# Attention and MLP in one kernel: the second half of each unit issues transposed score, score, score, transposed score

## The chip, the cores and the metric

The kernel runs on one core of a Trainium2 chip. The metric is the device time of one execution in microseconds (us). The median of three timed runs of the kernel before is 1475.2 us (1474.68 to 1475.99). All profile readings here are of one profiled execution; TensorE is called PE, VectorE DVE, ScalarE ACT, GpSimd POOL and SyncE SP, as the profile does.

## The reference

```
xn  = layernorm(x)                                   # x: 2048 x 512
q, k, v = split(xn @ wqkv)                           # 32 heads of 16
o   = softmax(q k^T / sqrt(16)) v                    # 2048 x 2048 per head
A   = o @ wo
B   = gelu(xn @ w1 + b1) @ w2 + b2                   # 1792 hidden
out = x + A + B
```

Attention needs each score tile twice, once for the row maximum and once transposed for the exponential. The projections, the MLP and the output projection are dense products that fill the gaps of attention.

## The kernel before

Attention is cut into 512 units: a group of four heads (8 groups), a block of 512 queries (4 blocks), and 16 steps in each. The function `unit` issues one step. The array of PE is used as eight tiles of 64 rows by 32 columns: each product of 512 columns is sent as four matmuls for the four column groups (`tiled`, L169), on the lower rows (0 to 63) or the upper rows (64 to 127). Head b of the four lies on the lower rows when b is even and on the upper rows when b is odd. So two streams run side by side in the array, and the order in which the program lists them decides what stands in front of what.

A unit has two halves, a = 0 and a = 1. Each half first issues a quartet, then one value product and some dense products. The names used from here on, with the tile name of the profile in brackets:

- Sb, score of head b (`s_half`, tile pS): four matmuls of 62 rows, whose result DVE reduces to row maxima (`s_max`, L363). It takes the next of three score banks of PSUM in turn.
- Tb, transposed score of head b (`e_half`, tile pT): four matmuls of 64 rows, whose result ACT turns into exponentials (L410, tile pe). It takes the next bank from the list T, which it shares with the dense groups: four banks in all, of which a dense group holds one (D). When one dense group ends and the next begins, both hold one for a while, and T has two left.
- V, the value product (`v_half`, tile pV): four fp32 matmuls, one per head, each shown as two passes in the trace. In the half a = 0 it uses the upper rows (and exponentials of two units before), in the half a = 1 the lower rows (of the unit before).
- D, the dense products (`dense`, tile pD): on the rows that V leaves free, three or four products in a half. The pair of numbers is a group's pace: FAST is (4, 4), SLOW is (3, 3), MEAN is (3, 4), by even and odd units. The 56 hidden groups of the MLP have 12 products each and alternate SLOW and FAST; the second matrix of the MLP has MEAN and then FAST; the projections are FAST.

The order of a quartet is a table of pairs (kind, b), kind 1 for T and 0 for S. Before, the first half issues T1 (upper), S0 (lower), S1 (upper), T0 (lower), and the second S2 (lower), T3 (upper), S3 (upper), T2 (lower). After the first quartet V goes to the upper rows and D to the lower; after the second V goes to the lower and D to the upper. PE's instructions stand in exactly this order; a semaphore wait stands on the first matmul of an S (for DVE to have emptied its bank) or of a T (for ACT). V's first product waits for the V and D of the half before (`turns`, set in `enter` and `leave`). A dense group ends after a half a = 1, so the instruction of ACT that empties its bank (hh at L1312 for the hidden layer, pf at L604 for the projections) is issued after the first quartet of the next unit and before the second (`one_more`). `s_end` and `stores` turn a block's maxima once in 16 units, through PE (L386) and a bank of T.

Of the kernel before, what the change touches and what calls it, by code (L numbers as in the profile page):

```python
# [54 lines left out]
def layer_kernel(ctx: ExitStack, tc: tile.TileContext, x, wqkv, wo, w1, b1, w2, b2, out):  # L55
# [122 lines left out]
    def leave(user, goes_on):  # L178

        p = newest.pop(user, None)  # L180
        if p is not None and goes_on:
            p.then_inc(turns, 1)
            tc.no_tile_sem_insts.add(p.ins.name)
            counted[0] += 1
            left.append(p)

    def enter():

        if left:
            goal[0] = f"turn{counted[0]}"  # L190
            for p in left:
                tc.add_to_no_dep_group(goal[0], p.ins)
            left.clear()
# [16 lines left out]
    def fetch_scale(m):  # L210

        scale_of[m] = nc.scalar.alloc_register(f"sexp{m}")
        nc.scalar.reg_load(scale_of[m], sexp[0:1, m:m + 1].bitcast(I32))

    class Plan:
# [7 lines left out]
        def add(self, engine, ns, fn, after=(), take=(), free=(), size=0, tail=0, gap=0):  # L223
            t = dict(gap=gap, e=engine, ns=ns, fn=fn, after=[a for a in after if a], take=take, free=free, size=size, tail=tail,
                     end=None, n=len(self.todo))
            for key in free:
                self.users.setdefault(key, []).append(t)
            self.todo.append(t)
            return t
# [89 lines left out]
    def tick():  # L319
        held[0] = pos[0] < NU and pos[0] % 16 == 0  # L320
        run_due()
        run_steps()
        slot[0] += 1
# [42 lines left out]
    def s_half(u, n):  # L366

        s = banks("S")
        s_mm(u, n, s)
        s_max(u, n, s)  # L370

    def s_end(u):

        t, i = divmod(u, 16)
        if i < 15:
            return
        g, qb = divmod(t, NQB)
        mneg = mnegs[t % 2]
        nc.vector.tensor_reduce(mneg[:, :16], mt_of[t].rearrange("p h t k -> p (h t) k"), axis=AX.X, op=ALU.max, negate=True)
        given("dve", 220)  # L380

        def store():

            pt = banks("T")
            for a in range(2):
                nc.tensor.matmul(pt[32 * a:32 * a + 32, :64], mneg[64 * a:64 * a + 64, :],  # L386
                                 ident[64 * a:64 * a + 64, 64 * a:64 * a + 64], start=True, stop=True)
            mhl = work.tile([64, 2, 64], F16, name="mhl", bufs=2)
            nc.vector.tensor_scalar_mul(mhl[:, 0], pt[:64, :64], 1.0 / MROW)
            nc.vector.scalar_tensor_tensor(mhl[:, 1], pt[:64, :64], 1.0 / MROW, mhl[:, 0], op0=ALU.mult, op1=ALU.subtract)  # L390
            given("dve", 300)
            for a in range(2):
                nc.sync.dma_start(m_d[t, :, :, 64 * a:64 * a + 64], mhl[32 * a:32 * a + 16])
            for h in range(4):
                m_rows(t, h)

        stores[t] = store

    def e_half(u, n):

        p, a = divmod(n, 2)
        t, kt = divmod(u, 16)
        g, qb = divmod(t, NQB)
        st = banks("T")
        r = slice(64 * a, 64 * a + 64)
        k0 = (kt % 4) * P
        tiled(None, st, kst[g % 2][kt // 4][r, p, k0:k0 + P], qst[g % 2][qb][r, p, :], True, True)
        pe = work.tile([P, QB], F32, name="pe", bufs=12)
        ptiles[u, n] = pe
        nc.scalar.activation(pe, st, AF.Exp, scale=scale_of[g // 2])  # L410
        given("act", 520)

    def v_half(u, a):

        t, kt = divmod(u, 16)
        g, qb = divmod(t, NQB)
        if kt == 0 and a == 0:
            pv_of[t] = hold("V", "S")
        pv = pv_of[t][0]
        r = slice(64 * a, 64 * a + 64)  # L420
        for h in (2, 3, 0, 1):
            c = (4 * g + h) * VW
            product("V", pv[32 * h:32 * h + 32, :], vv[r, kt, c:c + 32], ptiles[u, h][r],
                    start=(kt == 0 and a == 0), stop=(kt == 15 and a == 1))
# [233 lines left out]
    def ended(at_once=True):  # L658

        if cur[0] is not None and cur[0].over():  # L660
            done, cur[0] = cur[0], None
            ends.append(done.end)
            if at_once:
                settle()
# [5 lines left out]
    def one_more():  # L670

        if ends:
            ends.pop(0)()
        elif extras:
            extras.pop(0)()
# [10 lines left out]
    def dense(gen, side):  # L686

        f = group(gen)
        for _ in range(0 if f is None else f.pace[pos[0] % 2]):
            if not f.usable(side):  # L690
                return
            f.product(side)
# [25 lines left out]
    def spare(gen, side):  # L718

        if extra[0] is None and not spent[0]:  # L720
            f = next(gen, 0)
            spent[0] = f == 0
            extra[0] = Halves(f) if f else None
        if extra[0] is not None:
            extra[0].product(side)
            if extra[0].at == extra[0].n:
                extra[0] = None
# [17 lines left out]
    def unit(gen):  # L745


        u = pos[0]
        e = u - LEAD
        if e > 0 and e % (2 * NQB * 16) == 0 and e < NU:  # L750
            fetch_scale(e // (2 * NQB * 16))
        pos[0] += 1
        for a in range(2):
            for kind, b in ((1, 1), (0, 0), (0, 1), (1, 0)) if a == 0 else ((0, 2), (1, 3), (0, 3), (1, 2)):
                if kind and 0 <= e < NU:
                    e_half(e, b)
                elif not kind and u < NU:
                    s_half(u, b)
                elif not kind and u > NU:
                    spare(gen, b % 2)  # L760
            if e >= 0:
                one_more()
                enter()

                w, r = (e - 2, 1) if a == 0 else (e - 1, 0)
                live = 0 <= w < NU
                new = r == 0 and w % 16 == 0
                if live and not new:
                    v_half(w, r)
                dense(gen, 1 - r)  # L770
                if live and new:
                    v_half(w, r)

                for user, goes_on in (("V", live and not (r == 1 and w % 16 == 15)),
                                      ("D", cur[0] is not None and not cur[0].over())):
                    leave(user, goes_on)
                for k in backlog:
                    backlog[k] = max(0, backlog[k] - HALF)
                if live and r == 1:
                    v_end(w)  # L780
                ended(False)

            if a == 0 and u % 16 == 0 and u // 16 - 1 in stores:
                stores.pop(u // 16 - 1)()
        if u < NU:
            s_end(u)
        tick()
# [9 lines left out]
    with ExitStack() as st1:  # L797
# [252 lines left out]
        for w in (1, 0):  # L1050
# [5 lines left out]
            else:  # L1056
                a = add("POOL", 800, lambda wf=wf, i1=i1: nc.gpsimd.tensor_scalar(tl[wf], tl[wf], i1, 0.0, op0=ALU.mult, op1=ALU.add), [h])
                w_ready[w] = add("POOL", 1100, lambda wf=wf, hi=hi, lo=lo: nc.gpsimd.tensor_tensor(lo, tl[wf], hi, op=ALU.subtract), [a], free=[wf])
        a = add("DVE", 90, lambda: nc.vector.tensor_tensor(sexp[:, 0:1], fac0[:, 0:1], fac0[:, 1:2], op=ALU.mult), [chain])
        a = add("DVE", 90, lambda: nc.vector.tensor_scalar_mul(sexp[:, 0:1], sexp[:, 0:1], DH ** -0.5), [a])  # L1060
# [5 lines left out]
        a = add("DVE", 90, lambda: nc.vector.tensor_tensor(amv[:, 2:3], amv[:, 0:1], amv[:, 1:2], op=ALU.max), v_sum)  # L1066
# [3 lines left out]
        for i in range(2):  # L1070
# [6 lines left out]
            else:  # L1077
                b = add("POOL", 1240, lambda key=key: nc.gpsimd.tensor_scalar(
                    tl[key], tl[key], inv_v[:, 0:1], 0.0, op0=ALU.mult, op1=ALU.add), [h])
# [30 lines left out]
        a = add("DVE", 220, maxima, m_last)  # L1110
# [3 lines left out]
        def turn_m():  # L1114
            tl[mkey] = sb_tile(mkey)
            for k in range(2):
# [3 lines left out]
        a = add("PE", 300, turn_m, [a], take=[mkey])  # L1120
        a = add("DVE", 160, lambda: nc.vector.tensor_scalar_mul(mhl[:, 0], tl[mkey][:64, :64], 1.0 / MROW), [a])
        a = add("DVE", 160, lambda: nc.vector.scalar_tensor_tensor(mhl[:, 1], tl[mkey][:64, :64], 1.0 / MROW, mhl[:, 0],
                                                                   op0=ALU.mult, op1=ALU.subtract), [a], free=[mkey])
# [136 lines left out]
        while not spent[0] or more or cur[0] is not None:  # L1260
            unit(fil)
            if pos[0] > 16:
                more = next(pre, 0) != 0
# [150 lines left out]
    with ExitStack() as st3:  # L1414
# [45 lines left out]
        while pos[0] < NU + LEAD + 2:  # L1460
            more_stacks()
            unit(fil)
# [32 lines left out]
```

## Time and profile before

| | |
|---|---|
| median of three timed runs | 1475.2 us |
| the profiled execution, its own time | 1476.9 us |
| its span | 1475.1 us |
| granted clock | 0.997 |
| ACT busy | 1260.5 us (85%) |
| POOL busy | 662.4 us (45%) |

The span runs from the first to the last instruction, and 1.8 us of the execution's own time lie outside it. Units run from about 99 us to 1460 us. In a timeline each row has the start and the length of one or several instructions that follow each other ("x4"); for PE a row of four matmuls with tile pS is one score, with pT one transposed score, and x8 two of them that overlap. A PE row's length is longer than the time for which the array is taken, since matmuls are pipelined; the spacing of starts on the same rows tells that time.

### The profile page before, as it was taken

To read this page: it belongs to the slowest core of one execution; us is meant where nothing else is said; L and a number is where in the kernel's file an instruction comes from. 1 tells how busy PE (TensorE), PEld (TensorE's weight loads), DVE (VectorE), ACT (ScalarE), POOL (GpSimd) and SP (SyncE) were. 2 spreads that over 40 slices of the span, in tenths; PEclk is the share of its full clock that TensorE was granted. 3 is DMA by queue.
4 is the path that set the end of the run, shared out by engine and by line. 5 is a ranking of instruction groups with operands and counts; after the bars stand their busy time and mean duration, and the time that the engine had idled before them with its cause. 6 is when DMAs were issued, how large, how long until landed. Compare 5 with 4: busy or idle time off the path is not lost.

```text
span 1475.1 us, 88125 instructions
## 1 busy us (share of the span) xinstructions
PE 1458.9 (99%) x40158; PEld 817.6 (55%) x40158; DVE 1356.4 (92%) x2305; ACT 1260.5 (85%) x2366; POOL 662.4 (45%) x672
## 2 busy tenths in 40 slices
PE   8999999999999999999999999999999999999998
PEld 4445555565555555555555555555555555555554
DVE  7889999999999999999999999999999999999933
ACT  5868888888999888899988889998889999888884
POOL 3201847563778401287830138783115777121100
PEclk9999999999999999999999999999999999999999
DMA  7732455545224210221113111121112110221432
GB/s 214 225 117 69 151 186 172 169 159 159 78 59 128 66 34 25 70 61 41 45 43 87 30 37 44 51 76 44 44 37 76 55 37 21 57 55 31 142 94 96
DMA packets 112623, 124.83 MB, mean 85 GB/s; under 512 B 22908, under 2 KB 84220, under 8 KB 112248
## 3 DMA queue, kind: packets, MB, share of 16 engines
q1 hardware_dynamic: 112248, 119.18, 27.0%
q8 instruction: 314, 5.14, 1.4%
q14 instruction: 61, 0.50, 0.1%
HBM read 81.66 MB, written 37.34 MB: 81 GB/s over the span
## 4 chain that ended last, share of the span: by engine, by line
PE 95%; ACT 2%; DVE 1%; DMA 1%; issue 0%; SPq 0%; DVEq 0%; ACTq 0%
PE pV L169 29%; PE pD L169 25%; PE pT L169 19%; PE pS L169 19%; PE pT L992 2%; DMA wq<-in_A_wqkv_dram 1%; PE pD L992 1%; DVE mt L363 1%; ACT pe L410 0%; DVE ac L1370 0%; DMA m_d<-mhl 0%; PE pT L962 0%; ACT xs L945 0%; ACT hh L1312 0%; PE pS L1158 0%
## 5 line engine op out<-in xcount | busy, mean ns | idle before, releaser
L363 DVE TENSOR_REDUCE mt<-pS 128x1 f32<-128x512 f32 x2029 | 1278.9, 684 | 54.9 <-PE pS L169 27.0
L410 ACT ACTIVATE pe<-pT 128x512 f32<-128x512 f32 x2048 | 1111.4, 599 | 168.1 <-PE pS L169 79.8
L169 PE MATMUL pV<-pe,vv 64*32 64x512 f32 x8192 | 1074.3, 594 | 0.1
L169 PE MATMUL pT<-qst,kst 64*32 64x512 f16 x8192 | 707.4, 377 | 2.0 <-issue 1.3
L169 PE MATMUL pS<-kst,qst 62*32 62x512 f16 x8116 | 611.1, 378 | 1.2 <-DVE mt L363 1.2
L169 PEld LDWEIGHTS <-qst 62*32 62x32 f16 x8192 | 286.0, 92 | 228.9 <-issue 55.3
L169 PE MATMUL pD<-xb,wc 64*32 64x512 f16 x5376 | 362.1, 377 | 0.0
L169 PEld LDWEIGHTS <-kst 64*32 64x32 f16 x8192 | 276.1, 91 | 154.7 <-issue 62.1
L169 PE MATMUL pD<-w_s,g 64*32 64x512 f16 x5376 | 358.0, 377 | 0.0
L169 PEld LDWEIGHTS pV<-pe,vv 64*32 64x32 f32 x8192 | 182.3, 105 | 89.2 <-PE pV L169 4.2
L169 PE MATMUL pD<-xt,wqk_h 64*32 64x512 f16 x2400 | 158.7, 378 | 0.1
L169 PEld LDWEIGHTS <-wc 64*32 64x32 f16 x5376 | 117.2, 91 | 41.0 <-issue 0.7
L169 PEld LDWEIGHTS <-g 64*32 64x32 f16 x5376 | 114.5, 92 | 39.7 <-issue 0.3
L1337 POOL TENSOR_TENSOR xa<-xa,yt 128x512 f32<-128x512 f32 x16 | 20.5, 1280 | 226.8 <-ACT yt L1335 226.8
L466 POOL TENSOR_TENSOR osb<-osb,rb 128x512 f32<-128x512 f32 x31 | 39.8, 1284 | 165.3 <-DMA rb<-den_d 154.2
L1289 POOL TENSOR_TENSOR t<-hh 128x512 f32<-128x512 f32 x56 | 58.2, 1039 | 84.0 <-ACT hh L1312 83.1
L1291 POOL TENSOR_TENSOR t<-t,hh 128x512 f32<-128x512 f32 x56 | 71.8, 1282 | 4.7
L1284 POOL TENSOR_TENSOR t<-t,hh 128x512 f32<-128x512 f32 x56 | 71.7, 1281 | 4.7
L1286 POOL TENSOR_TENSOR g<-t,g 128x512 f16<-128x512 f32 x56 | 65.2, 1164 | 4.7
L1283 POOL TENSOR_SCALAR t<-t,gs 128x512 f32<-128x512 f32 x56 | 38.8, 693 | 63.3 <-ACT t L1278 63.3
L169 PEld LDWEIGHTS <-wqk_h 64*32 64x32 f16 x2400 | 54.4, 92 | 20.5 <-issue 2.3
L169 PE MATMUL pD<-wo_s,oc 64*32 64x512 f16 x828 | 54.5, 378 | 0.0
(160 smaller groups left out, 873.1 us busy)
## 6 DMA issues: line engine op xcount, KB each, us to landing
wc<-w_d SPq DMA_DIRECT2D x56, 256.0 KB
qk_d<-stg SPq DMA_DIRECT2D x32, 256.0 KB
rb<-den_d SPq DMA_DIRECT2D x124, 64.0 KB
wch<-in_B_w_dram SPq DMA_DIRECT2D x14, 512.0 KB
wch<-in_B_w_dram SPq DMA_DIRECT2D x28, 256.0 KB
w_d<-wsp SPq DMA_DIRECT2D x28, 256.0 KB
kst<-qk_d SPq DMA_DIRECT2D x64, 96.0 KB
qst<-qk_d SPq DMA_DIRECT2D x64, 96.0 KB
```

The source lines that it names most:

```text
L169: p = nc.tensor.matmul(*args, **kw)
L363: nc.vector.reduce_max(mt_of[t][:, n, qt, kb:kb + 1], s, axis=AX.X)
L410: nc.scalar.activation(pe, st, AF.Exp, scale=scale_of[g // 2])
L466: pooled((1280, lambda: nc.gpsimd.tensor_tensor(osb, osb, rb, op=ALU.mult)), (620, lambda: nc.gpsimd.tensor_scalar(ot[:, 0], osb, 1.0, 0.0 ...
L992: nc.tensor.matmul(tl[key], lhs, rhs, start=c + n == 0, stop=(c, n) == (NC - 1, 2))
L1283: pooled((690, lambda: nc.gpsimd.tensor_scalar(t1, t1, 1.0, gs[:, 1:2], op0=ALU.add, op1=ALU.mult)), (1280, lambda: nc.gpsimd.tensor_tenso ...
L1284: (1280, lambda: nc.gpsimd.tensor_tensor(t1, t1, hh, op=ALU.mult)),
L1286: (1160, lambda: nc.gpsimd.tensor_tensor(g[:, 1, f, :], t1, g[:, 0, f, :], op=ALU.subtract)),
L1289: pooled((1040, lambda: nc.gpsimd.tensor_tensor(t1, hh, hh, op=ALU.mult)), (620, lambda: nc.gpsimd.tensor_scalar(t1, t1, 1.0, 1.0 / GELU_A ...
L1291: (1280, lambda: nc.gpsimd.tensor_tensor(t1, t1, hh, op=ALU.mult)),
L1337: add = lambda: nc.gpsimd.tensor_tensor(xa, xa, yt, op=ALU.add)
```

## The change

```diff
--- before.py
+++ after.py
@@ -751,7 +751,7 @@
             fetch_scale(e // (2 * NQB * 16))
         pos[0] += 1
         for a in range(2):
-            for kind, b in ((1, 1), (0, 0), (0, 1), (1, 0)) if a == 0 else ((0, 2), (1, 3), (0, 3), (1, 2)):
+            for kind, b in ((1, 1), (0, 0), (0, 1), (1, 0)) if a == 0 else ((1, 2), (0, 3), (0, 2), (1, 3)):
                 if kind and 0 <= e < NU:
                     e_half(e, b)
                 elif not kind and u < NU:
```

The second quartet becomes T2 (lower), S3 (upper), S2 (lower), T3 (upper). The first is as it was.

On PE, a second quartet in the MLP's hidden layer stood so before (of the four matmuls of each only the first is shown; pS_20486 is S2, pT_20492 is T3, pS_20499 is S3, pT_20505 is T2):

```order
L169 MATMUL pD_20372<-xb_16070,wc_19873 32x512
...
L169 MATMUL pS_20486<-kst1_3_86,qst1_1_92 32x512 [waits DVE_49]
...
L169 MATMUL pT_20492<-qst1_0_91,kst1_2_85 32x512 [waits Activation_49]
...
L169 MATMUL pS_20499<-kst1_3_86,qst1_1_92 32x512 [waits DVE_49]
...
L169 MATMUL pT_20505<-qst1_0_91,kst1_2_85 32x512 [waits Activation_49]
...
L169 MATMUL pV_19867<-pe_20413,vv_95 32x512 [waits turns]
```

and in the change (pT_20486 is T2, pS_20493 is S3, pS_20499 is S2, pT_20505 is T3):

```order
L169 MATMUL pD_20372<-xb_16070,wc_19873 32x512
...
L169 MATMUL pT_20486<-qst1_0_91,kst1_2_85 32x512 [waits Activation_49]
...
L169 MATMUL pS_20493<-kst1_3_86,qst1_1_92 32x512 [waits DVE_49]
...
L169 MATMUL pS_20499<-kst1_3_86,qst1_1_92 32x512 [waits DVE_49]
...
L169 MATMUL pT_20505<-qst1_0_91,kst1_2_85 32x512 [waits Activation_49]
...
L169 MATMUL pV_19867<-pe_20394,vv_95 32x512 [waits turns]
```

A wait for ACT now stands ahead of both scores, the two scores are neighbours, and the transposed score that stands last lies on the upper rows instead of the lower.

On ACT, around the end of a hidden group (hh), the exponentials of T1 and T0 stand ahead of hh and those of the second quartet behind it. Before:

```order
L410 ACTIVATE pe_20643<-pT_20638 128x512 [waits PE_49,Activation_49]
L410 ACTIVATE pe_20662<-pT_20657 128x512 [waits PE_49]
L1312 ACTIVATE hh_20664<-pD_20372,b1_s_111 128x512 [waits Pool_49]
L410 ACTIVATE pe_20694<-pT_20689 128x512 [waits PE_49]
L410 ACTIVATE pe_20707<-pT_20702 128x512 [waits PE_49]
```

and in the change:

```order
L410 ACTIVATE pe_20643<-pT_20638 128x512 [waits PE_49,Activation_49]
L410 ACTIVATE pe_20662<-pT_20657 128x512 [waits PE_49,Activation_49]
L1312 ACTIVATE hh_20664<-pD_20372,b1_s_111 128x512 [waits Pool_49]
L410 ACTIVATE pe_20688<-pT_20683 128x512 [waits PE_49]
L410 ACTIVATE pe_20707<-pT_20702 128x512 [waits PE_49]
```

The exponential of T0, the second of each unit, now has two semaphores to wait for instead of one; the two behind hh are now of T2 and T3, in that order. The maxima on DVE are as many as before, with S3 ahead of S2.

## The prediction

> **What bounds the kernel now.** First the page: its list of busy times, its chain of waits, and three of its costliest groups.
>
> ```profile
> PE 1458.9 (99%) x40158; PEld 817.6 (55%) x40158; DVE 1356.4 (92%) x2305; ACT 1260.5 (85%) x2366; POOL 662.4 (45%) x672
> PE 95%; ACT 2%; DVE 1%; DMA 1%; issue 0%; SPq 0%; DVEq 0%; ACTq 0%
> L363 DVE TENSOR_REDUCE mt<-pS 128x1 f32<-128x512 f32 x2029 | 1278.9, 684 | 54.9 <-PE pS L169 27.0
> L410 ACT ACTIVATE pe<-pT 128x512 f32<-128x512 f32 x2048 | 1111.4, 599 | 168.1 <-PE pS L169 79.8
> L169 PE MATMUL pD<-xb,wc 64*32 64x512 f16 x5376 | 362.1, 377 | 0.0
> ```
>
> PE is always busy and carries the chain, DVE is next. A busy PE is not yet a full one, though: two streams share the array, and one can stand still while the other runs. That shows only in a timeline, from V to V. Here is a unit of a SLOW group (three dense products a half), by PE's timeline:
>
> ```profile
> 623.28 0.62 PE L169 MATMUL pV<-pe,vv 64*32 64x512 f32 x4
> 623.72 0.61 PE L169 MATMUL pV<-pe,vv 64*32 64x512 f32 x4
> ...
> 624.54 0.63 PE L169 MATMUL pV<-pe,vv 64*32 64x512 f32 x4
> 625.24 0.39 PE L169 MATMUL pS<-kst,qst 62*32 62x512 f16 x4
> 625.42 0.59 PE L169 MATMUL pT<-qst,kst 64*32 64x512 f16 x8
> 625.64 0.40 PE L169 MATMUL pS<-kst,qst 62*32 62x512 f16 x4
> 625.83 0.62 PE L169 MATMUL pV<-pe,vv 64*32 64x512 f32 x4
> ```
>
> V starts on the lower rows at 623.28, on the upper at 624.54, on the lower at 625.83. The half that ends with the first quartet takes 1.26 us, the one that ends with the second 1.29. By the program the first quartet has T, S, S, T with the rows in turn; the second has two upper-row pieces as neighbours (T3 at 625.42, the first of the x8, and S3 at 625.64).
>
> A FAST unit (four products a half), from the same view:
>
> ```profile
> 241.23 0.59 PE L169 MATMUL pV<-pe,vv 64*32 64x512 f32 x1
> 242.54 0.61 PE L169 MATMUL pV<-pe,vv 64*32 64x512 f32 x4
> 243.40 0.39 PE L169 MATMUL pT<-qst,kst 64*32 64x512 f16 x4
> 243.42 0.59 PE L169 MATMUL pS<-kst,qst 62*32 62x512 f16 x8
> 243.86 0.60 PE L169 MATMUL pV<-pe,vv 64*32 64x512 f32 x1
> ```
>
> Its halves take 1.31 and 1.32. Here both streams come out of V and D at about the same time (T3 at 243.40, S2 at 243.42) and are full.
>
> The third kind is the unit behind the end of a dense group. At the end of a FAST group, with a SLOW one behind it (PE, then ACT):
>
> ```profile
> 637.69 0.59 PE L169 MATMUL pV<-pe,vv 64*32 64x512 f32 x1
> 638.33 0.48 PE L169 MATMUL pS<-kst,qst 62*32 62x512 f16 x4
> 638.55 0.39 PE L169 MATMUL pT<-qst,kst 64*32 64x512 f16 x4
> 638.76 0.39 PE L169 MATMUL pS<-kst,qst 62*32 62x512 f16 x4
> 638.91 0.40 PE L169 MATMUL pT<-qst,kst 64*32 64x512 f16 x4
> 638.98 0.39 PE L169 MATMUL pD<-xb,wc 64*32 64x512 f16 x4
> 639.13 0.61 PE L169 MATMUL pV<-pe,vv 64*32 64x512 f32 x4
> 640.40 0.63 PE L169 MATMUL pV<-pe,vv 64*32 64x512 f32 x4
> ...
> 637.77 1.09 ACT L410 ACTIVATE pe<-pT 128x512 f32<-128x512 f32 x2 [0.24 <-PE pT L169]
> 638.74 0.69 ACT L1312 ACTIVATE hh<-pD,b_s 128x512 f32<-128x512 f32 x1
> ```
>
> T2, the last of the quartet, starts at 638.91, which is 0.05 behind the end of T0's exponential (637.77 + 1.09 = 638.86): with two banks left in T, it waits for the bank that T0 used. V on the lower rows stands behind T2 there and starts 0.22 later, so that this half takes 639.13 - 637.69 = 1.44.
>
> **The change part by part.** No instruction is added but one semaphore wait per unit on ACT; the quartet is reordered.
>
> *SLOW units, clean halves.* The new second quartet is the first with upper and lower exchanged: the free rows start with a T, the rows of V follow with an S, then S and T. So its price is that of the first quartet, 1.26 instead of 1.29, 0.03 less. The 5376 dense matmuls of the hidden layer are 5376 / (4 columns x 2 row halves) = 672 products, 56 groups of 12; 28 are SLOW and take four units each, one of which is the unit behind a group's end. 28 x 3 = 84 clean halves x 0.03 = 2.5 us. The bound below is nothing, if the 1.26 needs something that only the first quartet has. What sets 1.26 can be seen: from V's second pass at 623.72 to the next V at 624.54 it is 0.82, and `turns` makes V wait for the V and D before it, whatever the quartet's order.
>
> The eight pT at 625.42 hold T2, fourth in the program. They end at 625.42 + 0.59 = 626.01, and four of them alone last 0.39 (the pT of the FAST unit), so T2 runs from about 625.62, ahead of S3 at 625.64, third in the program: a piece whose rows are free passes one whose rows are not. The Trainium skill, page "TensorE: Matmul & The Clock Gate", section "Part 3: Packing small matmuls — row/col tiling", says that matmuls start and end strictly in program order; this trace differs by those rows. By the rule T2 would stand behind S3, V would come at about 625.86 as an estimate, and the same 84 halves would be worth 0.06 each, 5 us, which lies in the forecast's own range.
>
> *FAST units.* Over one unit each row half holds one V, one D of four products and two quartets' pieces, before and after alike, and both are full: 1.31 + 1.32 stays. Two quartets of one kind could round 0.01 up or down: with the MEAN units, at most 512 - 112 = 400 units x 0.01 = 4 us either way. I take nothing, as each row half's work is the same.
>
> *The unit behind a FAST group (28 times).* Now T2 stands first. Its bank comes from T1, whose exponential ends at 637.77 + 0.60 = 638.37 (two take 1.09, and start half a microsecond apart); with the same 0.05, T2 can start at 638.42, S3 on the upper rows at 638.55 as T3 did, S2 behind T2 at 638.63. T3 takes the bank of T0 and starts where T2 did, at 638.91, but on the upper rows. V's rows are then free at 638.84 and V waits only to be reached in the program: D, on rows that were free, started 0.07 behind T2's start, so V starts between 638.98 and 639.12 instead of 639.13. That is 0.01 to 0.15; I take 0.10, nearer to the row of D, since it is the same place in the program. D on the upper rows is now the late one, at 639.13, but has three products, and the half behind it is set by V. 28 x 0.10 = 2.8 us (bounds 0.3 to 4.2).
>
> *The unit behind a SLOW group.* The same exchange, but four products follow:
>
> ```profile
> 629.52 0.63 PE L169 MATMUL pV<-pe,vv 64*32 64x512 f32 x4
> 630.40 0.40 PE L169 MATMUL pT<-qst,kst 64*32 64x512 f16 x4
> 630.89 0.40 PE L169 MATMUL pT<-qst,kst 64*32 64x512 f16 x4
> 630.93 0.40 PE L169 MATMUL pD<-xb,wc 64*32 64x512 f16 x4
> 631.10 0.61 PE L169 MATMUL pV<-pe,vv 64*32 64x512 f32 x4
> 632.40 0.63 PE L169 MATMUL pV<-pe,vv 64*32 64x512 f32 x4
> ```
>
> V comes earlier than 631.10, but D on the upper rows comes at 630.89 + 0.22 = 631.11 instead of 630.93; four products of 0.22 and two pieces of 0.21 bring the next V to 631.11 + 0.88 + 0.42 = 632.41, against 632.40. Nothing gained. The switches of the projections, FAST on both sides, go the same way.
>
> *DVE.* The third score of a unit comes from the rows of V instead of the free ones, so in SLOW units about 0.2 later (625.42 instead of 625.24).
>
> ```profile
> 801.26 0.33 DVE L454 RECIPROCAL dn<-dn 64x32 f32<-64x32 f32 x1
> 801.52 5.01 DVE L363 TENSOR_REDUCE mt<-pS 128x1 f32<-128x512 f32 x8
> ```
>
> Eight maxima in 5.01 are 0.62 each or a little less, 2.48 for a unit of 1.26 + 1.26 = 2.52: covered, but with 0.04 to spare where there was 0.07. What DVE does beside, a reciprocal of 0.33 once in 16 units, is caught up more slowly. Of the 31, some 31 x 112 / 512 = 7 fall into SLOW units. If DVE set the pace outright there, 7 x 0.33 = 2.3 us would be lost, and nothing if the three banks cover it; I take 0.05 each, 0.4 us, since DVE's idle time after scores is but 27 of 1475 us now.
>
> *ACT's added wait*, on T0's exponential.
>
> ```profile
> 826.79 2.10 ACT L410 ACTIVATE pe<-pT 128x512 f32<-128x512 f32 x4
> ```
>
> Four exponentials in a row take 2.10, so with 0.60 for one (the page's 599 ns) they start (2.10 - 0.60) / 3 = 0.50 apart, and one of any four in a row already has two waits (T1's). I take nothing. If the wait forbade the overlap of 0.10, T0's bank would come 0.10 later at each of the 56 ends of hidden groups: 5.6 us, which is the bound above.
>
> Sum: -2.5 - 2.8 + 0.4 = -4.9. The profiled execution took 1476.9 (span 1475.1 and 1.8 around it), 1.7 above the median of the runs shown, 1475.2; it would come to 1472.0, and the median to **1470.3 us**.
>
> **The rivals.**
>
> *Nothing.* If V's 1.26 is not a property of the order, and the late D behind a FAST group gives back what V gains, 1475. For it: PE's busy share of 99%, and the FAST units. Against it: 1.26 and 1.29 in the same unit.
>
> *Slower: the T ahead holds the scores.* A T that waits for ACT now has both scores behind it in the program. The place is the unit in which the maxima are turned, when a dense group ends there too:
>
> ```profile
> 731.15 0.41 PE L169 MATMUL pS<-kst,qst 62*32 62x512 f16 x3
> 731.51 0.40 PE L169 MATMUL pT<-qst,kst 64*32 64x512 f16 x4
> 731.73 0.40 PE L169 MATMUL pS<-kst,qst 62*32 62x512 f16 x4
> ```
>
> Before, S2 started at 731.15 and T3 waited until 731.51; now S3 and S2 would wait with T2 for those 0.36. DVE, 92% busy, would stand, and what it loses comes back as late score banks. It decides once T1's exponential ends later than the free rows' slot, and in at most 31 units (512 / 16, less the first) it costs 31 x 0.36 = 11.2 us, less the 2.5 of the clean halves: 1484. Against it: elsewhere that exponential is in time (638.42 against a score at 638.55; 629.75 + 0.60 + 0.05 = 630.40 against 630.40, with nothing to spare).
>
> *The second half becomes like the first altogether.* Second halves behind a group's end take 1.44, or 631.10 - 629.52 = 1.58. If the waits went too, the 28 of the one kind would give 0.3 and the others of some 100 switches 0.1: 28 x 0.3 + 80 x 0.1 + 2.5 = 19, so 1456. Against it: ACT still empties the dense bank between the two quartets, and the last T still waits for it.
>
> **How the numbers follow.** The forecast has 0.52, nothing 0.25, the held scores 0.18, the full mirror 0.05. What a measurement can tell from no change is about 0.2%, 3 us. Of the forecast nine tenths lie below 1472.2 (0.47), with the mirror and a little of the second case 0.55 faster; 0.25 within 0.2%; 0.20 slower. Range: the low end is the sum with its best values, 2.5 + 4.2 + 4 = 10.7, so 1464; the high end takes ACT's bound on top of no gain, 1475 + 5.6, so 1480. The forecast's own range is 1466 to 1473.
>
> **What would show it.** In the changed timeline, SLOW units with both halves at 1.26; behind FAST groups V at least 0.05 ahead of a late D, and 1.3 to 1.4 for that half instead of 1.44; FAST units still 2.63 together; maxima on DVE in unbroken runs with no idle time named after pS above the 27 us of before. It is wrong if second halves stay at 1.29, if PE's rows show pS late behind a pT that waits for ACT, or if ACT's exponentials in a pair no longer overlap.

## The result, and the profile after

| | median | lowest to highest | runs |
|---|---|---|---|
| before | 1475.46 us | 1474.55 to 1477.44 | 10 |
| changed | 1471.73 us | 1469.05 to 1473.49 | 10 |

The ratio is 0.9972, with an interval of 0.9962 to 0.9982: 0.28% less time, or 3.7 us. The forecast was 1470.3. The profiled execution of the changed kernel has a span of 1469.8 us at a granted clock of 0.996, against 1475.1 at 0.997.

From the page of the changed kernel, the list of busy times, the chain of waits, and the groups of the row maxima and the exponentials:

```profile
PE 1451.9 (99%) x40158; PEld 837.9 (57%) x40158; DVE 1367.9 (93%) x2305; ACT 1259.1 (86%) x2366; POOL 662.5 (45%) x672
PE 95%; ACT 2%; DVE 1%; DMA 1%; issue 1%; SPq 0%; ACTq 0%; DVEq 0%
L363 DVE TENSOR_REDUCE mt<-pS 128x1 f32<-128x512 f32 x2029 | 1291.6, 684 | 37.6 <-PE pT L169 7.5
L410 ACT ACTIVATE pe<-pT 128x512 f32<-128x512 f32 x2048 | 1109.4, 598 | 164.4 <-PE pT L169 101.2
```

PE carries the chain as before. In the last two lines the number behind the second bar is the time in us that the engine stood idle ahead of the group. For the maxima it fell from 54.9 to 37.6, and it is no longer the scores that end most of it: maxima do not wait longer in the new order.

A unit of a SLOW group, PE's timeline of the changed kernel (start, length, instructions):

```profile
620.09 0.63 PE L169 MATMUL pV<-pe,vv 64*32 64x512 f32 x4
620.55 0.61 PE L169 MATMUL pV<-pe,vv 64*32 64x512 f32 x4
...
621.37 0.63 PE L169 MATMUL pV<-pe,vv 64*32 64x512 f32 x4
621.82 0.61 PE L169 MATMUL pV<-pe,vv 64*32 64x512 f32 x4
...
622.64 0.63 PE L169 MATMUL pV<-pe,vv 64*32 64x512 f32 x4
```

The halves are now alike, 621.37 - 620.09 = 1.28 and 622.64 - 621.37 = 1.27, together 2.55. Before they were 1.26 and 1.29, together 2.55. Nothing was gained here.

The unit behind a FAST group, with three products a half to follow (PE, then ACT):

```profile
634.94 0.59 PE L169 MATMUL pV<-pe,vv 64*32 64x512 f32 x3
...
635.23 0.47 PE L169 MATMUL pT<-qst,kst 64*32 64x512 f16 x4
635.36 0.54 PE L169 MATMUL pS<-kst,qst 62*32 62x512 f16 x8
635.71 0.40 PE L169 MATMUL pT<-qst,kst 64*32 64x512 f16 x4
635.76 0.63 PE L169 MATMUL pV<-pe,vv 64*32 64x512 f32 x4
635.93 0.61 PE L169 MATMUL pD<-xb,wc 64*32 64x512 f16 x8
636.22 0.61 PE L169 MATMUL pV<-pe,vv 64*32 64x512 f32 x4
...
637.04 0.63 PE L169 MATMUL pV<-pe,vv 64*32 64x512 f32 x4
```

```profile
634.58 1.09 ACT L410 ACTIVATE pe<-pT 128x512 f32<-128x512 f32 x2 [0.29 <-PE pT L169]
```

T3, now the last of the quartet, still waits for the exponential of T0 (634.58 + 1.09 = 635.67, T3 at 635.71). But it lies on the rows of D. V starts 0.05 behind it instead of 0.22 behind T2, and D is now the late one, at 635.93. V's second pass of the half before stands at 634.94, and 634.94 + 0.82 = 635.76: V is as early as `turns` lets it be.

The traces give this for every unit. A unit is counted here from the start of V on the upper rows to the next such start, its first half being the one that the second quartet ends, and sorted by what its dense products are. "Clean" units stand behind no end and have no maxima turned in them. Means in us, first and second half, worked out from the starts in the two traces:

```
                                          units  before        changed       sum of differences, us
SLOW hidden, behind an end, three follow     25  1.454+1.276   1.282+1.286   -4.05
  the same, maxima turned there               2  2.043+1.270   1.835+1.289   -0.38
behind an end, second matrix, three follow    4  1.424+1.269   1.259+1.276   -0.63
behind a SLOW hidden group, four follow      26  1.568+1.306   1.472+1.384   -0.46
behind an end, q and k projection            24  1.457+1.326   1.339+1.409   -0.82
SLOW hidden, clean                           80  1.299+1.218   1.287+1.234   +0.38
FAST hidden, clean                           52  1.363+1.297   1.328+1.323   -0.50
second matrix, four products, clean         106  1.357+1.297   1.349+1.310   +0.54
all units                                   511                              -5.1
```

Some small groups of units are left out of the rows. Of the 25 units of the first row, 23 stand behind a FAST hidden group and two behind the second matrix; of the two below, one and one; of the four of the second matrix, one stands behind a FAST hidden group. The second half of a clean SLOW unit was 1.26 before, as in the prediction's rows, but 1.14 in the last unit of a group, hence its mean of 1.218. The time came from the units behind the end of a dense group, above all from those in which three products follow.

### The profile page after: what moved, and what is told of

Same layout as the page of the kernel before. It is cut to its first block, busy times and chain, and to the rows that moved or that the text cites. A ratio compares the mean times of both kernels' runs of the same rounds, so it can differ in the third digit from the quotient of the medians.

```text
span 1469.8 us, 88641 instructions
## 1 busy us (share of the span) xinstructions
PE 1451.9 (99%) x40158; PEld 837.9 (57%) x40158; DVE 1367.9 (93%) x2305; ACT 1259.1 (86%) x2366; POOL 662.5 (45%) x672
## 4 chain that ended last, share of the span: by engine, by line
PE 95%; ACT 2%; DVE 1%; DMA 1%; issue 1%; SPq 0%; ACTq 0%; DVEq 0%
PE pV L169 28%; PE pD L169 27%; PE pT L169 20%; PE pS L169 18%; PE pT L992 2%; DMA wq<-in_A_wqkv_dram 1%; PE pD L992 1%; ACT pe L410 1%; DVE ac L1370 0%; ACT xs L945 0%; ACT wqk_h L881 0%; SPq L858 0%; PE pT L962 0%; ACT wch L881 0%; ACT xt L966 0%
## 5 line engine op out<-in xcount | busy, mean ns | idle before, releaser
L363 DVE TENSOR_REDUCE mt<-pS 128x1 f32<-128x512 f32 x2029 | 1291.6, 684 | 37.6 <-PE pT L169 7.5
L169 PE MATMUL pS<-kst,qst 62*32 62x512 f16 x8116 | 587.9, 378 | 1.3 <-DVE mt L363 1.2
L169 PEld LDWEIGHTS <-qst 62*32 62x32 f16 x8192 | 290.0, 91 | 237.2 <-issue 43.2
L169 PEld LDWEIGHTS <-kst 64*32 64x32 f16 x8192 | 269.3, 91 | 117.6 <-issue 28.1
L169 PEld LDWEIGHTS <-wc 64*32 64x32 f16 x5376 | 123.6, 91 | 46.9 <-issue 0.6
L169 PEld LDWEIGHTS <-g 64*32 64x32 f16 x5376 | 118.1, 92 | 41.4 <-issue 0.3
L169 PEld LDWEIGHTS <-wqk_h 64*32 64x32 f16 x2400 | 57.4, 92 | 22.7 <-issue 3.3
```

Source lines behind the costliest of these rows:

```text
L169: p = nc.tensor.matmul(*args, **kw)
L363: nc.vector.reduce_max(mt_of[t][:, n, qt, kb:kb + 1], s, axis=AX.X)
```

## The experiments

Every kernel below is the one before with one edit of the second quartet. They were timed in five rounds each, beside the kernel before.

**The new order only behind ends, and only elsewhere.** `ends` is the list of dense groups that have ended and not yet been emptied; it is not empty at the start of a unit that follows an end.

```diff
+        second = ((1, 2), (0, 3), (0, 2), (1, 3)) if ends else ((0, 2), (1, 3), (0, 3), (1, 2))
         for a in range(2):
-            for kind, b in ((1, 1), (0, 0), (0, 1), (1, 0)) if a == 0 else ((0, 2), (1, 3), (0, 3), (1, 2)):
+            for kind, b in ((1, 1), (0, 0), (0, 1), (1, 0)) if a == 0 else second:
```

> New order of the second quartet in the units behind the end of a dense group alone (some 110 of 512), old order elsewhere. Theory A (the gain is made behind group ends: the T that waits for ACT no longer lies on V's rows, and three products follow): nearly all of the gain, 5 us in the traces, so about 1470 and a ratio of 0.996 to 0.9975; units behind FAST groups take about 2.57 instead of 2.73. Theory B (the clean SLOW halves pay, as the prediction's first term had it): those stay as before, so at most the 2.8 us of the prediction's second term.

Measured: 1469.53 us, ratio 0.9956 (0.9943 to 0.997). In its trace the clean SLOW units stay at 2.517, and the 25 units of the table's first row take 2.577 instead of 2.730.

The complement has the two orders in that line exchanged.

> The complement: new order everywhere but behind group ends. Theory A: no gain, 1475 to 1477, ratio 1.000 to 1.001; units behind FAST groups keep 2.73; a clean SLOW unit keeps 2.55 in sum (its two halves 1.276 each instead of 1.264 and 1.289). Theory B: 2.5 us less, 1473.

Measured: 1476.6 us, ratio 1.0009 (0.9999 to 1.0019). In its trace the clean SLOW units take 1.287 + 1.230 = 2.517, before 2.517, though the halves are as in the changed kernel. So the whole gain lies behind the ends, and the clean SLOW halves give nothing. The kernel with the new order only behind ends is the fastest that was run; it beats the one before clearly, and the changed one by its median (1469.53 against 1471.73), while the intervals of the two ratios still overlap.

**Which of the two exchanges does it?** The change swaps two things at once: a T stands first instead of a score, and the last T lies on the rows of D instead of those of V. Two more orders, in all units, separate them. Score first, last T on the rows of D:

```diff
-            ... if a == 0 else ((0, 2), (1, 3), (0, 3), (1, 2)):
+            ... if a == 0 else ((0, 3), (1, 2), (0, 2), (1, 3)):
```

> Second quartet S3, T2, S2, T3 in all units: a score first as before, but the last T on the upper rows, those of D, as in the change. Theory A (the rows of the last T decide): the units behind FAST groups take about 2.57 as in the change, and the time is 1470 to 1473. Rival C (that a T stands ahead of the scores decides): they keep 2.73, and the time stays at 1475 or above.

Measured: 1470.4 us, ratio 0.9964 (0.9951 to 0.9978). And T first, last T on the rows of V:

```diff
-            ... if a == 0 else ((0, 2), (1, 3), (0, 3), (1, 2)):
+            ... if a == 0 else ((1, 3), (0, 2), (0, 3), (1, 2)):
```

> Second quartet T3, S2, S3, T2 in all units: a T first as in the change, but the last T on the lower rows, those of V, as before. Theory A: no gain, units behind FAST groups at 2.7 and more, 1475 to 1478. Rival C: the gain of the change, 1470 to 1473.

Measured: 1478.53 us, ratio 1.0011 (1.0 to 1.0022).

The same place in both traces. Score first, PE and then ACT:

```profile
635.34 0.40 PE L169 MATMUL pT<-qst,kst 64*32 64x512 f16 x4
635.36 0.38 PE L169 MATMUL pS<-kst,qst 62*32 62x512 f16 x1
635.39 0.63 PE L169 MATMUL pV<-pe,vv 64*32 64x512 f32 x3
635.56 0.39 PE L169 MATMUL pD<-xb,wc 64*32 64x512 f16 x3
```

```profile
634.21 1.09 ACT L410 ACTIVATE pe<-pT 128x512 f32<-128x512 f32 x2 [0.23 <-PE pT L169]
```

T first, but the last one on V's rows:

```profile
639.80 0.40 PE L169 MATMUL pT<-qst,kst 64*32 64x512 f16 x4
639.87 0.39 PE L169 MATMUL pD<-xb,wc 64*32 64x512 f16 x4
640.01 0.61 PE L169 MATMUL pV<-pe,vv 64*32 64x512 f32 x4
```

```profile
638.66 1.08 ACT L410 ACTIVATE pe<-pT 128x512 f32<-128x512 f32 x2 [0.30 <-PE pT L169]
```

In both the last T starts as soon as T0's exponential has ended (635.30 and 635.34; 639.74 and 639.80). With that T on D's rows V follows 0.05 later and D 0.22 later; with it on V's rows D follows 0.07 later and V 0.21 later. Over the 25 units the first half is 1.281 in the one and 1.448 in the other, against 1.454 before and 1.282 in the changed kernel. The row of the last T decides; what stands first does not.

**Only the 28 ends of FAST hidden groups, and only the others.** `ended` notes whether the group was a hidden one at FAST pace:

```diff
+            fast[0] = done.finish.__name__ == "hidden" and done.pace == FAST
...
+        second = ((1, 2), (0, 3), (0, 2), (1, 3)) if ends and fast[0] else ((0, 2), (1, 3), (0, 3), (1, 2))
```

> New order only behind the 28 hidden groups of FAST pace, where three products a half follow. Theory A (V's path is shortened, and it counts only where D has slack): 28 x 0.15 to 0.18 = 4.2 to 5.0 us less, so 1470.5 to 1471.5, ratio 0.9965 to 0.9975. Rival G (any unit behind a group end gains): 28 of some 110 such units, a quarter of 6 us, so 1474.

Measured: 1471.53 us, ratio 0.9975 (0.9966 to 0.9984). The complement has `ends and not fast[0]`.

> The complement among group ends: new order behind all other group ends (hidden SLOW, second matrix, projections). Theory A: little, 0.5 to 1.5 us less, most of it where MEAN groups go on with three: 1474 to 1475. Rival G: three quarters of 6 us, 1471.

Measured: 1473.47 us, ratio 0.9986 (0.9977 to 0.9995). The 28 ends give 0.25%, all others (some 85 units) 0.14%; together 0.39%, against 0.44% for both at once, within the intervals.

**Could the last T leave V's way altogether?** If V waits for its place behind T3 in the program, T3 issued behind V should free it. This starts from the kernel with the new order only behind ends: `behind` is true in units behind an end, which have the new order; there the quartet leaves T3 out, and it follows V:

```diff
-                    e_half(e, b)
+                    if not (behind and b == 3):
+                        e_half(e, b)
...
                     v_half(w, r)
+                if behind and a == 1 and e < NU:
+                    e_half(e, 3)
                 dense(gen, 1 - r)
```

> As the kernel with the new order behind group ends alone (1469.5), and there T3 is issued behind V and ahead of the dense products. Theory A now says that V in these units is set by its wait for the V before it (0.82 behind its second pass), no longer by T3: nothing more to gain, 1468.5 to 1471, half still 1.26 behind FAST groups. Rival D (V still waits for its place behind T3, which the trace shows starting 0.05 ahead of it): V up to 0.1 earlier in some 100 units where it is not set by the wait, 1462 to 1467.

Measured: 1477.05 us, ratio 1.0013 (1.0005 to 1.0022). Neither theory had foreseen a loss. PE's timeline at the same place:

```profile
638.44 0.59 PE L169 MATMUL pV<-pe,vv 64*32 64x512 f32 x1
...
639.26 0.63 PE L169 MATMUL pV<-pe,vv 64*32 64x512 f32 x4
639.30 0.40 PE L169 MATMUL pT<-qst,kst 64*32 64x512 f16 x4
639.52 0.39 PE L169 MATMUL pD<-xb,wc 64*32 64x512 f16 x4
639.72 0.60 PE L169 MATMUL pV<-pe,vv 64*32 64x512 f32 x3
...
640.61 0.62 PE L169 MATMUL pV<-pe,vv 64*32 64x512 f32 x4
```

V starts at 639.26 = 638.44 + 0.82, no earlier than in the changed kernel: T3 had not been holding it. T3 now starts behind V, at 639.30, although its bank was free: in this trace T0's exponential ends at 638.09 + 1.08 = 639.17.

```profile
638.09 1.08 ACT L410 ACTIVATE pe<-pT 128x512 f32<-128x512 f32 x2 [0.24 <-PE pT L169]
```

By the 0.05 of the other traces it would have started at 639.22. On the upper rows there follow three products, T1 and S1, six pieces with T3. From T3 to the next V at 640.61 it is 1.31, or 0.218 for each of the six, and T3 and the product behind it start 639.52 - 639.30 = 0.22 apart: the rows are full, and `turns` would have let V start at 639.72 + 0.82 = 640.54. So the free rows have little slack: in the changed kernel six pieces of 0.218 from 635.71 would end at 637.02, and the next V is at 637.04. Over the 25 units the second half is 1.348, against 1.286. Where four products follow it is worse: the 24 units of the q and k projection behind an end take 2.911 instead of 2.782, 3.1 us in all.

With T3 behind V and D:

```diff
                 dense(gen, 1 - r)
...
                     v_half(w, r)
+                if behind and a == 1 and e < NU:
+                    e_half(e, 3)
```

> As before, with T3 issued behind V and all the dense products of that half. Theory A: behind SLOW groups, where four products follow, the late D is what keeps the unit at 2.87, and taking T3 out of its way gives 0.10 to 0.15 in some 28 to 80 units: 1458 to 1467. Rival F: T3's exponential, 0.9 late, holds the next unit's T banks and gives it back: 1469 or more.

Measured: 1479.79 us, ratio 1.0028 (1.0017 to 1.0039). Theory A's gain behind SLOW groups did not come: the 26 units take 2.879, before 2.874. The second halves behind an end are as long as with T3 behind V (1.345, and the projection's units 2.910), and clean units lose too: the 80 of SLOW groups 1.2 us, the 52 of FAST groups 0.7 against before, or 1.3 against the -0.6 that nearly every other kernel has there. A late exponential that holds the banks of T for the next unit, the expectation's rival F, fits this; which bank waits for which was not followed through, so it is not shown.

## Why the prediction was right, and where it was wrong

**The sum came out near the forecast, with other terms.** The prediction had -2.5 for clean SLOW halves, -2.8 behind FAST groups, +0.4 on DVE, and nothing elsewhere. Measured: 3.7 us less. That the sum came this near is partly luck: the first term gave nothing, and the ends of groups gave more than they had been counted for.

**Clean SLOW halves, -2.5: the failed step.** It reads "its price is that of the first quartet, 1.26 instead of 1.29". The second quartet was indeed no longer at 1.29, but the first was no longer at 1.26. In five kernels with four different second quartets the two halves of the 80 clean units come to 2.516 to 2.521 on average. The 1.26 was no property of a quartet but a gift of the one before it: by the prediction's own rows the 1.26 began with a first pass of V of 623.72 - 623.28 = 0.44, and the 1.29 was 624.99 - 624.54 = 0.45 and 625.83 - 624.99 = 0.84. In the changed kernel both first passes take 0.45 to 0.46 (620.09 to 620.55, 621.37 to 621.82), with 0.82 behind each. The 0.84 did fall to 0.82, but the next half's 0.44 rose by as much: what one half saved, the other paid. Its lower bound, "nothing, if the 1.26 needs something that only the first quartet has", is what happened. Where the last T lies on D's rows the first halves are 1.287 on average, where it lies on V's rows 1.299 or 1.300, with the same sum; what in the array makes a first pass 0.01 shorter stays open.

**The rule on program order.** T2 passed S3 in the rows of before, by which the Trainium skill's rule (page "TensorE: Matmul & The Clock Gate", section "Part 3: Packing small matmuls — row/col tiling": starts and ends strictly in program order) did not hold across the row halves. What the prediction worked out from it, 5 us over the same halves, was not found either. Its rows behind a FAST group show a wider passing, of 0.15: D starts at 638.98, and V, which stands ahead of it in the program, at 639.13. By `turns` V could have gone from 638.12 + 0.82 = 638.94 on, so it lacked only its rows, which T2 had from 638.91. In the trace of before D is ahead in 23 of the table's 25 units of the first row by 0.12 to 0.17 (in the other two the program itself lists D first); in the changed kernel it is behind V in all.

**Behind a FAST group, -2.8: right in mechanism, too small.** T3 starts where T2 did, on D's rows, V comes ahead of D, and three products leave room for a late D: all as said, but for three of the 28 units, where four products of the second matrix follow; these gave 0.1 us together. The term took 0.10 per unit, between 0.01 and 0.15. In the trace of the changed kernel, where three follow, the half falls by 0.17 and the next one grows by 0.01, so 0.16 a unit; all 28 are 4.2 us shorter. The kernel with the edit at these 28 ends alone gained 0.25% (0.16 to 0.34), 3.7 us or 0.13 each (0.08 to 0.18). The prediction put V between D's place in the program and T2's end; what set it was `turns`, 0.82 behind V's second pass, at 0.05 behind T3. From this follows the most that any order could give in these halves, as long as `turns` waits for V and D: before, the half was 1.44, and 0.44 + 0.82 = 1.26 is the shortest.

**Other ends: taken as nothing, worth about 2 us.** Behind SLOW hidden groups it was as worked out: V gains 0.10 in one half, and D gives back 0.08 in the next, 0.5 us over 26 units (0.1 us in the two kernels that have the order there and keep the old one in clean units). The units of the second matrix that have three products to follow, left out of the sum, gained 0.16 each; the projections, where four follow, kept 0.03 of 0.12.

**FAST units, taken as even:** 0.5 us more over 106 units of the second matrix and 0.5 less over 52 of the hidden layer, either way 0.01 a unit. The second of these is no gain of the order: the kernel with the new order elsewhere, which has it in these units, and the one behind ends, which has not, both show -0.6, so it belongs to the one trace of before. **DVE, +0.4:** clean SLOW units show +0.38 in the changed kernel but +0.11 in the kernel that has the same order in these units and the old one behind ends, so no loss is shown. **ACT's added wait:** exponentials in a pair still take 1.09, as before.

**The slower rival, the T ahead holding the scores, did not come:** DVE's idle time fell, and the two SLOW units in which the maxima are turned behind an end became 0.19 shorter. At the place that the rival named, where four products follow, the unit stayed at 3.3 (2.02 + 1.30 before, 1.80 + 1.50 in the changed kernel). And the order with the score first (0.9951 to 0.9978) can't be told from the changed one (0.9962 to 0.9982). **Nothing** failed because the late D gives back only where four products follow. **The full mirror** was half right: V's half behind an end did fall to 1.28, but the row that V left became the late one, as that rival's counter-argument had it.

The changed kernel gains less than its edit behind the ends alone. In its trace clean units in which the maxima are turned are longer (the five in SLOW groups 2.801 instead of 2.738, +0.32; with the old order in them, +0.06), and the clean SLOW and second-matrix units are 0.9 longer together. That these make up the 2.2 us between the medians is not shown.

## What to carry to other kernels

Where two streams share the array and the last piece ahead of them must wait, put that piece on the rows of the stream with slack, here the one with three products rather than the value product that sets the half; where neither has slack the wait only moves into the next half. Before a half is taken as the price of its own order, add it to its neighbour: two unequal halves can be one fixed sum. And an instruction moved behind the one that it seems to hold should first be shown to hold it.

## What had not been expected of the hardware

- A transposed score whose bank is ready by 639.22 (639.17 and the usual 0.05) starts at 639.30 when a value product on the other rows, started at 639.26, stands ahead of it in the program. So passing, as T2 passed S3 and D passed V before, is not to be counted on. In these rows a piece passed one that lacked only its rows, and did not pass one that still waited by `turns`; that this decides was not tested by a run of its own.
- The first of the two passes of the fp32 value product took 0.44 in one half of a SLOW unit before, 0.45 in the other, and 0.45 to 0.46 in both halves of the changed kernel. From the second pass to the next V it was 0.82, and 0.84 behind the old second quartet.
- In the last unit of a dense group `turns` has V alone to wait for, and the next V starts 0.70 behind the second pass (626.35 - 625.65 in the changed kernel; so in all 26 such units among the 80 clean SLOW ones before, and 0.82 in 50 of the other 54). Yet where both are waited for, D is done before V: its third product ends at 620.57 + 0.39 = 620.96, V's at 620.55 + 0.61 = 621.16. Why waiting for both takes 0.12 more stays open.
